# An attention-then-FFN kernel on one core: 512-token FFN tiles, one load queue in the order of need, v scaled on VectorE at first, scores inside the y step

## The chip, the cores and the metric

One core of one Trainium2 chip. The metric is the device time of one execution in microseconds (us), as the median of several runs. The traced span is 1.7 us shorter than the time of the same run (276.9 and 278.6 for the kernel before), so times are compared with times and spans with spans.

The names: PE is TensorE (the matmul engine), ACT is ScalarE, DVE is VectorE, POOL is GpSimd, SP is SyncE. A queue is the list of transfers that one engine issues; a transfer lands when its last data are in the core. Half clock is a stretch in which PE was granted about 0.5 of its full clock.

## The reference

A recurrent attention with a fixed decay per head, then a gated FFN over its output. Shapes: 4 batches, 8 heads, 768 positions, head size 64 (so 3072 tokens of width 512), inner width 1536, all float32.

```python
def _attn_ref(q, k, v):
    gamma = 1.0 - 2.0 ** (-5.0 - np.arange(H))
    for t in range(S):
        state = gamma * state + outer(k[:, :, t], v[:, :, t])     # (B,H,D,D)
        y[:, :, t] = scale * einsum('bhd,bhde->bhe', q[:, :, t], state)

def _moe_ref(x, w_gate, w_val, w_out):
    gate = 1.0 / (1.0 + np.exp(-(x @ w_gate)))
    return (gate * (x @ w_val)) @ w_out
```

The kernels process attention in chunks of 128 positions (6 per batch, 24 in all): scores within a chunk, a state carried from chunk to chunk, the decay put into scaled v on one side and into a table on the other.

## The kernel before

Per chunk there are three steps: `step_t` (k and q transposed on PE, copied by ACT), `step_s` (scores, masked by VectorE), `step_y` (state z, output y, evicted by VectorE with the decay table). Attention of batch b+1 is dealt out between the FFN groups of batch b. What matters is the first part: which queue gets which load, in which order, and where v is scaled.

```python
def load_chunk(b, c):                       # k, q cast to bf16 on POOL's queue, v as f32 on SyncE's
    ...
    nc.gpsimd.dma_start(out=kn[b, c], in_=k[b, :, rows, :]...)
    nc.gpsimd.dma_start(out=qn[b, c], in_=q[b, :, rows, :]...)
    nc.sync.dma_start(out=vf[b, c], in_=v[b, :, rows, :]...)      # 8 buffers of vf

def scale_v(b, c):
    vs[b, c] = ld.tile([C, H, D], BF16, tag="vs", name="vs", bufs=8)
    nc.gpsimd.tensor_tensor(vs[b, c], vf[b, c], tabv[...], op=ALU.mult)
...
for c in range(NCH): load_chunk(0, c)       # (cut: constants and tables between them)
for s in range(NFF // 2): load_gate_val(s)  # w_gate and w_val, 256 columns each, POOL's queue
for s in range(4): load_out(s)
for c in range(NCH): scale_v(0, c)          # POOL again: strictly behind its 28 DMA issues
for c in range(NCH): load_chunk(1, c)
for step in attention(0): step()            # six chunks before the first FFN group
for b in range(B):
    groups = ffn_groups(b)                  # 24 up groups of 384 columns, 6 down groups
    steps = attention(b + 1) if b + 1 < B else []
    ...                                     # scale_v(b + 1, ...), load_chunk(b + 2, ...)
    for i, g in enumerate(groups):
        g()
        upto = -(-len(steps) * (i + 1) // len(groups))
        while done < min(upto, len(steps)): steps[done](); done += 1
```

Of the kernel before, what the change touches and what calls it, by code (L numbers as in the profile page):

```python
# [9 lines left out]
F32 = mybir.dt.float32  # L10
BF16 = mybir.dt.bfloat16
I32 = mybir.dt.int32
AX = mybir.ActivationFunctionType
# [4 lines left out]
def kernel(  # L18
# [19 lines left out]
    HALF = S // 2  # L38
# [12 lines left out]

    qn, kn, vf = {}, {}, {}

    def load_chunk(b, c):
        rows = slice(c * C, (c + 1) * C)
        qn[b, c] = ld.tile([C, H, D], BF16, tag="qn", name="qn")
        kn[b, c] = ld.tile([C, H, D], BF16, tag="kn", name="kn")
        vf[b, c] = ld.tile([C, H, D], F32, tag="vf", name="vf", bufs=8)
        nc.gpsimd.dma_start(out=kn[b, c], in_=k[b, :, rows, :].rearrange("h s d -> s h d"))  # L59
        nc.gpsimd.dma_start(out=qn[b, c], in_=q[b, :, rows, :].rearrange("h s d -> s h d"))  # L60
        nc.sync.dma_start(out=vf[b, c], in_=v[b, :, rows, :].rearrange("h s d -> s h d"))
# [5 lines left out]
    def load_gate_val(s):  # L67
        cols = slice(s * 256, (s + 1) * 256)
        for dst, src in ((wg, moe_w_gate), (wv, moe_w_val)):
            nc.gpsimd.dma_start(out=dst[:, :, cols],  # L70
                                in_=src.rearrange("(kk p) n -> p kk n", p=128)[:, :, cols])

    def load_out(s):
# [3 lines left out]

    tokv = const.tile([128, NCH], I32, name="tokv")
    nc.gpsimd.iota(tokv, pattern=[[C, NCH]], base=0, channel_multiplier=1)
    ident = const.tile([128, 128], BF16, name="ident")  # L80
    make_identity(nc, ident)
    load_chunk(0, 0)
    toky = const.tile([128, S], I32, name="toky")
    nc.gpsimd.iota(toky, pattern=[[1, S]], base=0, channel_multiplier=0)  # L84
# [3 lines left out]
                            compare_op=ALU.is_ge, fill=0.0)  # L88

# [14 lines left out]
    for p in range(NP):  # L104
        nc.scalar.activation(taby[:, p, :], toky, AX.Exp, scale=lgp[:, p:p + 1], bias=lsc)
# [4 lines left out]
    for c in range(1, NCH):  # L110
        load_chunk(0, c)


    xT, vs, qkT, stA, stB, zps, zbd = {}, {}, {}, {}, {}, {}, {}

    def scale_v(b, c):
        vs[b, c] = ld.tile([C, H, D], BF16, tag="vs", name="vs", bufs=8)
        nc.gpsimd.tensor_tensor(vs[b, c], vf[b, c],  # L118
                                tabv[:, c, :].unsqueeze(2).to_broadcast([C, H, D]), op=ALU.mult)

    def step_t(b, c):
        tp = pa.tile([128, 2 * NP, C], BF16, tag="tp", name="tp")
        for i, src in enumerate((kn[b, c], qn[b, c])):
            for p in range(NP):
                nc.tensor.transpose(tp[:, i * NP + p, :],  # L125
                                    src[:, 2 * p:2 * p + 2, :].rearrange("s h d -> s (h d)"), ident)
        qkT[b, c] = at.tile([128, 2 * NP, C], BF16, tag="qkT", name="qkT")
        nc.scalar.activation(qkT[b, c], tp, AX.Copy)  # L128

    def step_s(b, c):  # L130
        t = qkT[b, c]
        sA = pa.tile([128, NP, C], F32, tag="sA", name="sA")
        sB = pa.tile([128, NP, C], F32, tag="sB", name="sB")
        for p in range(NP):
            nc.tensor.matmul(sA[:, p, :], t[0:D, p, :], t[0:D, NP + p, :], start=True, stop=True)  # L135
            nc.tensor.matmul(sB[:, p, :], t[D:128, p, :], t[D:128, NP + p, :], start=True, stop=True)  # L136
        stA[b, c] = at.tile([128, NP, C], BF16, tag="stA", name="stA")
        stB[b, c] = at.tile([128, NP, C], BF16, tag="stB", name="stB")
        nc.vector.tensor_tensor(stA[b, c], sA, causal4, op=ALU.mult)  # L139
        nc.vector.tensor_tensor(stB[b, c], sB, causal4, op=ALU.mult)  # L140

    def step_y(b, c):
        t = qkT[b, c]
        if c == 0:
            xT[b] = at.tile([128, NP, S], BF16, tag="xT", name="xT")
            zps[b] = pa.tile([128, NP, C], F32, tag="z", name="z")
        if c < NCH - 1:
            for p in range(NP):
                nc.tensor.matmul(zps[b][:, p, :],  # L149
                                 kn[b, c][:, 2 * p:2 * p + 2, :].rearrange("s h d -> s (h d)"),  # L150
                                 vs[b, c][:, 2 * p:2 * p + 2, :].rearrange("s h d -> s (h d)"),
                                 start=(c == 0 and p == 0), stop=True, skip_group_check=True)
        y = pa.tile([128, NP, C], F32, tag="y", name="y")
        if c > 0:
            for p in range(NP):
                nc.tensor.matmul(y[:, p, :], zbd[b, c - 1][:, p, :], t[:, NP + p, :],  # L156
                                 start=(p == 0), stop=False, skip_group_check=True)
        for p in range(NP):
            nc.tensor.matmul(y[0:D, p, :], vs[b, c][:, 2 * p, :], stA[b, c][:, p, :],  # L159
                             start=(c == 0 and p == 0), stop=True, skip_group_check=True)  # L160
            nc.tensor.matmul(y[D:128, p, :], vs[b, c][:, 2 * p + 1, :], stB[b, c][:, p, :],  # L161
                             start=(c == 0 and p == 0), stop=True, skip_group_check=True)
        if c < NCH - 1:
            zbd[b, c] = at.tile([128, NP, C], BF16, tag="zbd", name="zbd")
            nc.vector.tensor_tensor(zbd[b, c], zps[b], diag4, op=ALU.mult)  # L165
        cols = slice(c * C, (c + 1) * C)
        nc.vector.tensor_tensor(xT[b][:, :, cols], y, taby[:, :, cols], op=ALU.mult)  # L167

    def attention(b):
        steps = [lambda: step_t(b, 0), lambda: step_s(b, 0)]  # L170
        for c in range(NCH):
            if c + 1 < NCH:
                steps.append(lambda c=c: step_t(b, c + 1))
            steps.append(lambda c=c: step_y(b, c))
            if c + 1 < NCH:
                steps.append(lambda c=c: step_s(b, c + 1))
        return steps


    def ffn_groups(b):  # L180
        hT = ffn.tile([128, NFF, S], BF16, tag="hT", name="hT", bufs=2)

        def up(n1, hf):
            cols = slice(hf * HALF, (hf + 1) * HALF)
            ps = []
            for w in (wg, wv):
                t = pf.tile([128, 512], F32, tag="ff", name="ff")
                for kk in range(KT):
                    nc.tensor.matmul(t[:, 0:HALF], w[:, kk, n1 * 128:(n1 + 1) * 128], xT[b][:, kk, cols],  # L189
                                     start=(kk == 0), stop=(kk == KT - 1))  # L190
                ps.append(t)
            gs = ffn.tile([128, HALF], F32, tag="gs", name="gs")
            nc.scalar.activation(gs, ps[0][:, 0:HALF], AX.Sigmoid)  # L193
            nc.vector.tensor_tensor(hT[:, n1, cols], gs, ps[1][:, 0:HALF], op=ALU.mult)  # L194

        def down(sm):
            o = pf.tile([128, 512], F32, tag="ff", name="ff")
            for n1 in range(NFF):
                nc.tensor.matmul(o, hT[:, n1, sm * 128:(sm + 1) * 128], wo[:, n1, :],  # L199
                                 start=(n1 == 0), stop=(n1 == NFF - 1))  # L200
            ob = ffn.tile([128, D_MODEL], F32, tag="ob", name="ob")
            nc.scalar.copy(ob, o)  # L202
            row = b * S + sm * 128
            nc.sync.dma_start(out=out[row:row + 128, :], in_=ob)

        return ([lambda n1=n1, hf=hf: up(n1, hf) for n1 in range(NFF) for hf in range(2)]
                + [lambda sm=sm: down(sm) for sm in range(NCH)])


    for s in range(NFF // 2):  # L210
        load_gate_val(s)
    for s in range(4):
        load_out(s)
    for c in range(NCH):
        scale_v(0, c)
    for c in range(NCH):
        load_chunk(1, c)
    for step in attention(0):
        step()
    for b in range(B):  # L220
        groups = ffn_groups(b)
        steps = attention(b + 1) if b + 1 < B else []
        if b + 1 < B:
            for c in range(NCH):
                scale_v(b + 1, c)
        if b + 2 < B:
            for c in range(NCH):
                load_chunk(b + 2, c)
        done = 0
        for i, g in enumerate(groups):  # L230
            g()
            upto = -(-len(steps) * (i + 1) // len(groups))
            while done < min(upto, len(steps)):
                steps[done]()
                done += 1
# [30 lines left out]
```

## Time and profile before

| | before |
|---|---|
| time, median of 3 runs | 277.68 us (277.05 to 278.29) |
| traced span | 276.9 us |
| first FFN matmul | 51.1 us |
| PE waits for data after it | 2.4 us, then half clock |
| one batch (FFN beside attention) | 56.97 us of PE |

How to read it: the page gives busy tenths per engine in 40 equal slices, the chain of waits follows the last instruction back to what released it, the waits sum up who stood idle for whom. The prediction below shows the lines.

### The profile page before, as it was taken

To read this page: it belongs to the slowest core of one execution; us is meant where nothing else is said; L and a number is where in the kernel's file an instruction comes from. 1 tells how busy PE (TensorE), PEld (TensorE's weight loads), DVE (VectorE), ACT (ScalarE), POOL (GpSimd) and SP (SyncE) were. 2 spreads that over 40 slices of the span, in tenths; PEclk is the share of its full clock that TensorE was granted. 3 is DMA by queue.
4 is the path that set the end of the run, shared out by engine and by line. 5 is a ranking of instruction groups with operands and counts; after the bars stand their busy time and mean duration, and the time that the engine had idled before them with its cause. 6 is when DMAs were issued, how large, how long until landed. Compare 5 with 4: busy or idle time off the path is not lost.

```text
span 276.9 us, 4474 instructions
## 1 busy us (share of the span) xinstructions
PE 233.9 (84%) x1792; PEld 136.2 (49%) x1792; DVE 110.1 (40%) x200; ACT 91.4 (33%) x158; POOL 80.6 (29%) x98
## 2 busy tenths in 40 slices
PE   0400058599999999999999999999999999999994
PEld 0200046355666544566666445666665455665441
DVE  1100049546555512356567112656761314444100
ACT  6310014234444312444443214444243124333121
POOL 8836599359892970041011000000000000000000
PEclk9999999979999999999999999999999999999999
DMA  9999999999990999680000122000001220000122
GB/s 135 183 157 182 196 199 195 160 158 176 178 133 8 65 169 147 161 144 0 2 1 0 69 85 76 2 0 2 1 2 38 78 96 20 2 0 0 38 96 96
DMA packets 86293, 23.89 MB, mean 86 GB/s; under 512 B 75520, under 2 KB 83200, under 8 KB 86272
## 3 DMA queue, kind: packets, MB, share of 16 engines
q0 software_dynamic: 57856, 11.01, 47.8%
q1 hardware_dynamic: 28416, 12.59, 20.3%
q8 instruction: 14, 0.23, 0.4%
q14 instruction: 7, 0.06, 0.1%
HBM read 28.31 MB, written 6.29 MB: 125 GB/s over the span
## 4 chain that ended last, share of the span: by engine, by line
PE 79%; DMA 12%; POOL 7%; issue 1%; ACT 0%; POOLq 0%; ACTq 0%
PE ff L189 46%; PE ff L199 23%; DMA qn<-in_q_dram 9%; DMA wg<-in_moe_w_gate_dram 4%; PE tp L125 3%; POOL vs L118 2%; PE y L159 2%; PE sA L135 2%; POOL kn L59 2%; PE y L156 1%; PE z L149 1%; POOL qn L60 1%; POOL wo L74 1%; POOL wv L70 1%; POOL toky L84 0%
## 5 line engine op out<-in xcount | busy, mean ns | idle before, releaser
L194 DVE TENSOR_TENSOR hT<-gs,ff 128x384 bf16<-128x384 f32 x96 | 53.1, 554 | 75.2 <-PE ff L189 57.6
L189 PE MATMUL ff<-xT,wg 128*128 128x384 bf16 x384 | 79.1, 329 | 0.0
L189 PE MATMUL ff<-xT,wv 128*128 128x384 bf16 x384 | 78.8, 328 | 0.0
L193 ACT ACTIVATE gs<-ff 128x384 f32<-128x384 f32 x96 | 47.0, 489 | 78.6 <-PE ff L189 47.8
L199 PE MATMUL ff<-wo,hT 128*128 128x512 bf16 x288 | 64.4, 379 | 0.0
L189 PEld LDWEIGHTS <-wv 128*128 128x128 bf16 x384 | 37.8, 98 | 25.2 <-issue 0.7
L189 PEld LDWEIGHTS <-wg 128*128 128x128 bf16 x384 | 34.9, 98 | 22.6 <-issue 0.5
L199 PEld LDWEIGHTS <-hT 128*128 128x128 bf16 x288 | 27.3, 98 | 31.9
L128 ACT ACTIVATE qkT<-tp 128x1024 bf16<-128x1024 bf16 x24 | 24.6, 1023 | 48.0 <-PE tp L125 48.0
L118 POOL TENSOR_TENSOR vs<-vf,tabv 128x512 bf16<-128x512 f32 x24 | 24.4, 1042 | 45.4 <-PE y L161 17.3
L202 ACT COPY ob<-ff 128x512 f32<-128x512 f32 x24 | 14.0, 585 | 53.7 <-PE ff L199 51.7
L165 DVE TENSOR_TENSOR zbd<-z,diag 128x512 bf16<-128x512 f32 x20 | 13.7, 684 | 40.7 <-PE z L149 40.7
L149 PE MATMUL z<-vs,kn 128*128 128x128 bf16 x80 | 8.2, 228 | 23.7 <-POOL vs L118 23.7
L59 POOL DMA_DIRECT2D kn<-in_k_dram x24 | 22.0, 915 | 6.0 <-DMA kn<-in_k_dram 3.6
L60 POOL DMA_DIRECT2D qn<-in_q_dram x24 | 21.6, 902 | 5.3 <-DMA qn<-in_q_dram 3.6
L139 DVE TENSOR_TENSOR stA<-sA,causal 128x512 bf16<-128x512 f32 x24 | 16.4, 683 | 16.5 <-PE sB L136 16.5
L167 DVE TENSOR_TENSOR xT<-y,taby 128x512 bf16<-128x512 f32 x24 | 16.4, 682 | 14.5 <-PE y L161 14.5
L149 PEld LDWEIGHTS <-kn 128*128 128x128 bf16 x80 | 6.3, 103 | 26.1 <-issue 23.9
L125 PE MATMUL tp<-ident,kn 128*128 128x128 bf16 x96 | 10.0, 230 | 8.0 <-DMA kn<-in_k_dram 8.0
L140 DVE TENSOR_TENSOR stB<-sB,causal 128x512 bf16<-128x512 f32 x24 | 16.3, 679 | 0.0
L125 PE MATMUL tp<-ident,qn 128*128 128x128 bf16 x96 | 10.2, 233 | 4.1 <-DMA qn<-in_q_dram 4.1
L125 PEld LDWEIGHTS <-kn 128*128 128x128 bf16 x96 | 7.2, 102 | 11.2 <-DMA kn<-in_k_dram 8.3
(34 smaller groups left out, 108.8 us busy)
## 6 DMA issues: line engine op xcount, KB each, us to landing
vf<-in_v_dram SPq DMA_DIRECT2D x24, 256.0 KB, 8.9
out_dram<-ob SPq DMA_DIRECT2D x24, 256.0 KB, 2.0
kn<-in_k_dram POOLq DMA_DIRECT2D x24, 128.0 KB, 8.5
qn<-in_q_dram POOLq DMA_DIRECT2D x24, 128.0 KB, 8.5
wg<-in_moe_w_gate_dram POOLq DMA_DIRECT2D x6, 256.0 KB, 10.1
wv<-in_moe_w_val_dram POOLq DMA_DIRECT2D x6, 256.0 KB, 10.0
wo<-in_moe_w_out_dram POOLq DMA_DIRECT2D x4, 384.0 KB, 13.2
```

The costliest lines, as they stand in the source:

```text
L59: nc.gpsimd.dma_start(out=kn[b, c], in_=k[b, :, rows, :].rearrange("h s d -> s h d"))
L60: nc.gpsimd.dma_start(out=qn[b, c], in_=q[b, :, rows, :].rearrange("h s d -> s h d"))
L118: nc.gpsimd.tensor_tensor(vs[b, c], vf[b, c], tabv[:, c, :].unsqueeze(2).to_broadcast([C, H, D]), op=ALU.mult)
L125: nc.tensor.transpose(tp[:, i * NP + p, :], src[:, 2 * p:2 * p + 2, :].rearrange("s h d -> s (h d)"), ident)
L128: nc.scalar.activation(qkT[b, c], tp, AX.Copy)
L139: nc.vector.tensor_tensor(stA[b, c], sA, causal4, op=ALU.mult)
L149: nc.tensor.matmul(zps[b][:, p, :], kn[b, c][:, 2 * p:2 * p + 2, :].rearrange("s h d -> s (h d)"), vs[b, c][:, 2 * p:2 * p + 2, :].rearran ...
L167: nc.vector.tensor_tensor(xT[b][:, :, cols], y, taby[:, :, cols], op=ALU.mult)
L189: nc.tensor.matmul(t[:, 0:HALF], w[:, kk, n1 * 128:(n1 + 1) * 128], xT[b][:, kk, cols], start=(kk == 0), stop=(kk == KT - 1))
L193: nc.scalar.activation(gs, ps[0][:, 0:HALF], AX.Sigmoid)
L194: nc.vector.tensor_tensor(hT[:, n1, cols], gs, ps[1][:, 0:HALF], op=ALU.mult)
L199: nc.tensor.matmul(o, hT[:, n1, sm * 128:(sm + 1) * 128], wo[:, n1, :], start=(n1 == 0), stop=(n1 == NFF - 1))
```

## The change

Its intent: start the FFN after four chunks of attention, not six; bring in each piece of data just before it is needed; keep the scaling of v off POOL's queue of DMA issues while that is long; put the scores of the next chunk inside the y step. The core of the diff:

```diff
+    def load_chunk(g):                     # g counts chunks over all batches
+        load_kq(g)
+        load_v(g, nc.gpsimd)               # v now on POOL's queue too
...
+    for g in range(4):
+        load_v(g, nc.sync)                 # only v of chunks 0 to 3 stays on SyncE's queue
+    load_kq(0) ... load_kq(3)              # (cut: constants between them)
...
+        eng = nc.vector if g < 8 else nc.gpsimd       # in step_t(g)
+        eng.tensor_tensor(vs[g], vf[g], tabv[...], op=ALU.mult)
...
-    def step_y(b, c):
+    def step_y(g, nxt=None):               # z, first half of y, then:
+        evict = step_s(nxt) if nxt is not None else None
...                                         # second half of y, evictions
-        def up(n1, hf):                    # 24 groups of 384 columns per batch
+        def up(n1):                        # 12 groups of 512 columns per tile of four chunks
...
-    for s in range(NFF // 2):
+    for s in range(3):
         load_gate_val(s)
+    load_chunk(4)
+    for s in range(3, NFF // 2):
+        load_gate_val(s)
+    load_chunk(5)
     for s in range(4):
         load_out(s)
-    for c in range(NCH):
-        scale_v(0, c)
-    for c in range(NCH):
-        load_chunk(1, c)
-    for step in attention(0):
+    load_chunk(6)
+    load_chunk(7)
+    first = attention(0)                   # chunks 0 to 3
+    first[0]()
+    for p in range(NP):
+        make_taby(p)                       # decay tables on ACT, behind the first copy
+    for step in first[1:]:
         step()
```

More of the change, by code (lines that the diff above doesn't have):

```diff
@@ L37 @@
     NFF = D_FF // 128
-    HALF = S // 2
     scale = 1.0 / math.sqrt(D)
@@ L49, with src, load_v, load_kq @@
     pf = ctx.enter_context(tc.tile_pool(name="pf", bufs=3, space=bass.MemoryType.PSUM))
+    NG = B * NCH
+    NT = N_TOK // 512
     qn, kn, vf = {}, {}, {}
-    def load_chunk(b, c):
-        rows = slice(c * C, (c + 1) * C)
-        qn[b, c] = ld.tile([C, H, D], BF16, tag="qn", name="qn")
-        kn[b, c] = ld.tile([C, H, D], BF16, tag="kn", name="kn")
-        vf[b, c] = ld.tile([C, H, D], F32, tag="vf", name="vf", bufs=8)
-        nc.gpsimd.dma_start(out=kn[b, c], in_=k[b, :, rows, :].rearrange("h s d -> s h d"))
-        nc.gpsimd.dma_start(out=qn[b, c], in_=q[b, :, rows, :].rearrange("h s d -> s h d"))
-        nc.sync.dma_start(out=vf[b, c], in_=v[b, :, rows, :].rearrange("h s d -> s h d"))
+    def src(x, g):
+        b, c = divmod(g, NCH)
+        return x[b, :, c * C:(c + 1) * C, :].rearrange("h s d -> s h d")
+    def load_v(g, eng):
+        vf[g] = ld.tile([C, H, D], F32, tag="vf", name="vf", bufs=8)
+        eng.dma_start(out=vf[g], in_=src(v, g))
+    def load_kq(g):
+        kn[g] = ld.tile([C, H, D], BF16, tag="kn", name="kn")
+        qn[g] = ld.tile([C, H, D], BF16, tag="qn", name="qn")
+        nc.gpsimd.dma_start(out=kn[g], in_=src(k, g))
+        nc.gpsimd.dma_start(out=qn[g], in_=src(q, g))
+    def load_chunk(g):
+        load_kq(g)
+        load_v(g, nc.gpsimd)
     wg = wpool.tile([128, KT, D_FF], BF16, name="wg")
@@ L68, in load_gate_val @@
         cols = slice(s * 256, (s + 1) * 256)
-        for dst, src in ((wg, moe_w_gate), (wv, moe_w_val)):
+        for dst, w in ((wg, moe_w_gate), (wv, moe_w_val)):
             nc.gpsimd.dma_start(out=dst[:, :, cols],
-                                in_=src.rearrange("(kk p) n -> p kk n", p=128)[:, :, cols])
+                                in_=w.rearrange("(kk p) n -> p kk n", p=128)[:, :, cols])
     def load_out(s):
@@ L75, in load_out @@
                             in_=moe_w_out.rearrange("(n p) d -> p n d", p=128)[:, s * 3:(s + 1) * 3, :])
+    for g in range(4):
+        load_v(g, nc.sync)
+    load_kq(0)
+    ident = const.tile([128, 128], BF16, name="ident")
+    make_identity(nc, ident)
+    load_kq(1)
     tokv = const.tile([128, NCH], I32, name="tokv")
     nc.gpsimd.iota(tokv, pattern=[[C, NCH]], base=0, channel_multiplier=1)
-    ident = const.tile([128, 128], BF16, name="ident")
-    make_identity(nc, ident)
-    load_chunk(0, 0)
-    toky = const.tile([128, S], I32, name="toky")
-    nc.gpsimd.iota(toky, pattern=[[1, S]], base=0, channel_multiplier=0)
     causal = const.tile([128, 128], F32, name="causal")
@@ L88 @@
                             compare_op=ALU.is_ge, fill=0.0)
+    load_kq(2)
+    toky = const.tile([128, S], I32, name="toky")
+    nc.gpsimd.iota(toky, pattern=[[1, S]], base=0, channel_multiplier=0)
+    load_kq(3)
     tabv = const.tile([128, NCH, H], F32, name="tabv")
@@ L103, with make_taby @@
     taby = const.tile([128, NP, S], F32, name="taby")
-    for p in range(NP):
+    def make_taby(p):
         nc.scalar.activation(taby[:, p, :], toky, AX.Exp, scale=lgp[:, p:p + 1], bias=lsc)
@@ L108, with pair, step_t, step_s @@
     diag4 = diag.unsqueeze(1).to_broadcast([128, NP, 128])
-    for c in range(1, NCH):
-        load_chunk(0, c)
-    xT, vs, qkT, stA, stB, zps, zbd = {}, {}, {}, {}, {}, {}, {}
-    def scale_v(b, c):
-        vs[b, c] = ld.tile([C, H, D], BF16, tag="vs", name="vs", bufs=8)
-        nc.gpsimd.tensor_tensor(vs[b, c], vf[b, c],
-                                tabv[:, c, :].unsqueeze(2).to_broadcast([C, H, D]), op=ALU.mult)
-    def step_t(b, c):
+    xT, vs, qkT, stA, stB, zbd = {}, {}, {}, {}, {}, {}
+    zps = {}
+    def pair(t, p):
+        return t[:, 2 * p:2 * p + 2, :].rearrange("s h d -> s (h d)")
+    def step_t(g):
         tp = pa.tile([128, 2 * NP, C], BF16, tag="tp", name="tp")
-        for i, src in enumerate((kn[b, c], qn[b, c])):
+        for i, x in enumerate((kn[g], qn[g])):
             for p in range(NP):
-                nc.tensor.transpose(tp[:, i * NP + p, :],
-                                    src[:, 2 * p:2 * p + 2, :].rearrange("s h d -> s (h d)"), ident)
-        qkT[b, c] = at.tile([128, 2 * NP, C], BF16, tag="qkT", name="qkT")
-        nc.scalar.activation(qkT[b, c], tp, AX.Copy)
-    def step_s(b, c):
-        t = qkT[b, c]
+                nc.tensor.transpose(tp[:, i * NP + p, :], pair(x, p), ident)
+        qkT[g] = at.tile([128, 2 * NP, C], BF16, tag="qkT", name="qkT")
+        nc.scalar.activation(qkT[g], tp, AX.Copy)
+        vs[g] = ld.tile([C, H, D], BF16, tag="vs", name="vs", bufs=4)
+        eng = nc.vector if g < 8 else nc.gpsimd
+        eng.tensor_tensor(vs[g], vf[g], tabv[:, g % NCH, :].unsqueeze(2).to_broadcast([C, H, D]),
+                          op=ALU.mult)
+    def step_s(g):
+        t = qkT[g]
         sA = pa.tile([128, NP, C], F32, tag="sA", name="sA")
@@ L136, in step_s, with evict @@
             nc.tensor.matmul(sB[:, p, :], t[D:128, p, :], t[D:128, NP + p, :], start=True, stop=True)
-        stA[b, c] = at.tile([128, NP, C], BF16, tag="stA", name="stA")
-        stB[b, c] = at.tile([128, NP, C], BF16, tag="stB", name="stB")
-        nc.vector.tensor_tensor(stA[b, c], sA, causal4, op=ALU.mult)
-        nc.vector.tensor_tensor(stB[b, c], sB, causal4, op=ALU.mult)
-    def step_y(b, c):
-        t = qkT[b, c]
+        stA[g] = at.tile([128, NP, C], BF16, tag="stA", name="stA")
+        stB[g] = at.tile([128, NP, C], BF16, tag="stB", name="stB")
+        def evict():
+            nc.vector.tensor_tensor(stA[g], sA, causal4, op=ALU.mult)
+            nc.vector.tensor_tensor(stB[g], sB, causal4, op=ALU.mult)
+        return evict
+    def step_y(g, nxt=None):
+        b, c = divmod(g, NCH)
+        if g % 4 == 0:
+            xT[g // 4] = at.tile([128, NP, 512], BF16, tag="xT", name="xT")
         if c == 0:
-            xT[b] = at.tile([128, NP, S], BF16, tag="xT", name="xT")
             zps[b] = pa.tile([128, NP, C], F32, tag="z", name="z")
@@ L148, in step_y @@
             for p in range(NP):
-                nc.tensor.matmul(zps[b][:, p, :],
-                                 kn[b, c][:, 2 * p:2 * p + 2, :].rearrange("s h d -> s (h d)"),
-                                 vs[b, c][:, 2 * p:2 * p + 2, :].rearrange("s h d -> s (h d)"),
+                nc.tensor.matmul(zps[b][:, p, :], pair(kn[g], p), pair(vs[g], p),
                                  start=(c == 0 and p == 0), stop=True, skip_group_check=True)
@@ L155, in step_y @@
             for p in range(NP):
-                nc.tensor.matmul(y[:, p, :], zbd[b, c - 1][:, p, :], t[:, NP + p, :],
+                nc.tensor.matmul(y[:, p, :], zbd[g - 1][:, p, :], qkT[g][:, NP + p, :],
                                  start=(p == 0), stop=False, skip_group_check=True)
+        evict = step_s(nxt) if nxt is not None else None
         for p in range(NP):
-            nc.tensor.matmul(y[0:D, p, :], vs[b, c][:, 2 * p, :], stA[b, c][:, p, :],
+            nc.tensor.matmul(y[0:D, p, :], vs[g][:, 2 * p, :], stA[g][:, p, :],
@@ L160, in step_y @@
                              start=(c == 0 and p == 0), stop=True, skip_group_check=True)
-            nc.tensor.matmul(y[D:128, p, :], vs[b, c][:, 2 * p + 1, :], stB[b, c][:, p, :],
+            nc.tensor.matmul(y[D:128, p, :], vs[g][:, 2 * p + 1, :], stB[g][:, p, :],
                              start=(c == 0 and p == 0), stop=True, skip_group_check=True)
         if c < NCH - 1:
-            zbd[b, c] = at.tile([128, NP, C], BF16, tag="zbd", name="zbd")
-            nc.vector.tensor_tensor(zbd[b, c], zps[b], diag4, op=ALU.mult)
@@ L166, in step_y @@
-        cols = slice(c * C, (c + 1) * C)
-        nc.vector.tensor_tensor(xT[b][:, :, cols], y, taby[:, :, cols], op=ALU.mult)
-    def attention(b):
-        steps = [lambda: step_t(b, 0), lambda: step_s(b, 0)]
-        for c in range(NCH):
-            if c + 1 < NCH:
-                steps.append(lambda c=c: step_t(b, c + 1))
-            steps.append(lambda c=c: step_y(b, c))
-            if c + 1 < NCH:
-                steps.append(lambda c=c: step_s(b, c + 1))
-        return steps
-    def ffn_groups(b):
-        hT = ffn.tile([128, NFF, S], BF16, tag="hT", name="hT", bufs=2)
-        def up(n1, hf):
-            cols = slice(hf * HALF, (hf + 1) * HALF)
+            zbd[g] = at.tile([128, NP, C], BF16, tag="zbd", name="zbd")
@@ new lines, in step_y, with attention @@
+            nc.vector.tensor_tensor(zbd[g], zps[b], diag4, op=ALU.mult)
+        if evict:
+            evict()
+        col = (g % 4) * C
+        nc.vector.tensor_tensor(xT[g // 4][:, :, col:col + C], y, taby[:, :, c * C:(c + 1) * C], op=ALU.mult)
+    def attention(t):
+        g = 4 * t
+        return [lambda: step_t(g), lambda: step_s(g)(), lambda: step_t(g + 1), lambda: step_y(g, g + 1),
+                lambda: step_t(g + 2), lambda: step_y(g + 1, g + 2), lambda: step_t(g + 3),
+                lambda: step_y(g + 2, g + 3), lambda: step_y(g + 3)]
@@ L185, in up, with ffn_groups @@
+    def ffn_groups(t):
+        hT = ffn.tile([128, NFF, 512], BF16, tag="hT", name="hT", bufs=2)
+        def up(n1):
             ps = []
             for w in (wg, wv):
-                t = pf.tile([128, 512], F32, tag="ff", name="ff")
+                u = pf.tile([128, 512], F32, tag="ff", name="ff")
                 for kk in range(KT):
-                    nc.tensor.matmul(t[:, 0:HALF], w[:, kk, n1 * 128:(n1 + 1) * 128], xT[b][:, kk, cols],
+                    nc.tensor.matmul(u, w[:, kk, n1 * 128:(n1 + 1) * 128], xT[t][:, kk, :],
@@ L190, in up @@
                                      start=(kk == 0), stop=(kk == KT - 1))
-                ps.append(t)
-            gs = ffn.tile([128, HALF], F32, tag="gs", name="gs")
-            nc.scalar.activation(gs, ps[0][:, 0:HALF], AX.Sigmoid)
-            nc.vector.tensor_tensor(hT[:, n1, cols], gs, ps[1][:, 0:HALF], op=ALU.mult)
+                ps.append(u)
+            gs = ffn.tile([128, 512], F32, tag="gs", name="gs")
+            nc.scalar.activation(gs, ps[0], AX.Sigmoid)
+            nc.vector.tensor_tensor(hT[:, n1, :], gs, ps[1], op=ALU.mult)
@@ L202, in down @@
             nc.scalar.copy(ob, o)
-            row = b * S + sm * 128
+            row = t * 512 + sm * 128
             nc.sync.dma_start(out=out[row:row + 128, :], in_=ob)
-        return ([lambda n1=n1, hf=hf: up(n1, hf) for n1 in range(NFF) for hf in range(2)]
-                + [lambda sm=sm: down(sm) for sm in range(NCH)])
-    for s in range(NFF // 2):
+        return [lambda n1=n1: up(n1) for n1 in range(NFF)] + [lambda sm=sm: down(sm) for sm in range(4)]
+    for s in range(3):
         load_gate_val(s)
+    load_chunk(4)
+    for s in range(3, NFF // 2):
+        load_gate_val(s)
+    load_chunk(5)
     for s in range(4):
         load_out(s)
-    for c in range(NCH):
-        scale_v(0, c)
-    for c in range(NCH):
-        load_chunk(1, c)
-    for step in attention(0):
-        step()
-    for b in range(B):
-        groups = ffn_groups(b)
-        steps = attention(b + 1) if b + 1 < B else []
-        if b + 1 < B:
-            for c in range(NCH):
-                scale_v(b + 1, c)
-        if b + 2 < B:
-            for c in range(NCH):
-                load_chunk(b + 2, c)
+    load_chunk(6)
[5 more added lines that the diff above has]
+    for step in first[1:]:
+        step()
+    for t in range(NT):
+        groups = ffn_groups(t)
+        steps = attention(t + 1) if t + 1 < NT else []
+        if t + 2 < NT:
+            for g in range(4 * t + 8, 4 * t + 12):
+                load_chunk(g)
         done = 0
-        for i, g in enumerate(groups):
-            g()
+        for i, group in enumerate(groups):
+            group()
             upto = -(-len(steps) * (i + 1) // len(groups))
```

## The prediction

> **What bounds the kernel now.** I read the busy slices of the page first, then the chain of work that ended last, then the waits, then the order of time on POOL, last the table of stretches. The slices:
>
> ```profile
> PE   0400058599999999999999999999999999999994
> POOL 8836599359892970041011000000000000000000
> PEclk9999999979999999999999999999999999999999
> DMA  9999999999990999680000122000001220000122
> ```
>
> A slice is 6.9 us. PE is full from the ninth slice on; before that it is nearly idle while the transfers are full. So there are two stages: some 55 us of start, bound by what is loaded and in which order, and 220 us bound by PE. The chain shows PE's stage and its unit costs:
>
> ```profile
> 43.38 11.91 DMA qn<-in_q_dram
> ...
> 112.58 1.30 PE ff L189 x8
> ...
> 169.55 1.30 PE ff L189 x8
> ...
> 226.52 31.20 PE ff L189 x192
> 257.72 15.55 PE ff L199 x72
> ...
> 273.34 0.58 ACT ob L202
> ```
>
> The last batch runs without attention beside it: 31.20/192 = 0.1625 us per 384-column up matmul, 15.55/72 = 0.216 us per 512-column down matmul, 46.75 us per batch. The pieces at 112.58 and 169.55 begin two successive batches: 56.97 us apart, of which 46.75 is FFN, so six chunks of attention take 10.2 us of PE, 1.70 each. What fills the start is in the waits:
>
> ```profile
> PE z L149 <- POOL vs L118: 23.7, 1, 23.7
> ...
> PE tp L125 <- DMA kn<-in_k_dram: 8.0, 2, 7.3
> ...
> PE tp L125 <- DMA qn<-in_q_dram: 4.1, 3, 1.7
> ```
>
> and on POOL, in order of time:
>
> ```profile
> 34.31 0.76 POOL L74 DMA_DIRECT2D wo<-in_moe_w_out_dram  x1 [0.58 <-DMA wg<-in_moe_w_gate_dram]
> 35.65 0.77 POOL L74 DMA_DIRECT2D wo<-in_moe_w_out_dram  x1 [0.58 <-DMA wv<-in_moe_w_val_dram]
> 36.44 6.04 POOL L118 TENSOR_TENSOR vs<-vf,tabv 128x512 bf16<-128x512 f32 x6
> ```
>
> The first v was in the core at 4.1 us (the trace records each landing), but its scaling stands behind 28 DMA issues in POOL's strict order and starts at 36.4. PE waits 23.7 us for it, runs attention of six chunks from 37.6 to 51.1, does one FFN group, then waits 0.63 and 1.74 us for chunk 0 of the next batch, queued behind all weights, and runs at half clock after that wait. The stretches give the transfer rates and the clock:
>
> ```profile
> 16.00:20.00 4.00, 0.00 (x0) 0.00 (x0) 0.00 (x0) 0.00 (x0) 1.36 (x3) 1.00 1.69 158
> 32.00:36.00 4.00, 0.00 (x0) 0.00 (x0) 0.00 (x0) 0.00 (x0) 2.24 (x4) 1.00 1.45 196
> 56.00:60.00 4.00, 4.00 (x23) 1.95 (x22) 1.42 (x3) 1.74 (x3) 1.36 (x3) 0.65 1.69 157
> ```
>
> The last two columns but one are clock and DMA share, the last GB/s: 158 with k, q and v beside each other, 196 with weights alone, clock 0.65 after the wait.
>
> Check of the model: first FFN group 51.1, FFN 768 x 0.1625 + 288 x 0.216 = 187.0, attention 18 x 1.70 = 30.6, waits 2.4, slow clock some 1.4, tail from 273.3 to 276.9 = 3.6. Sum 276.1 against 276.9 seen.
>
> **What the Trainium skill says.** (1) "TensorE: Matmul & The Clock Gate", section "Wait — 56ns, not 53.3ns?": warm, a matmul of N columns costs N/2.4 GHz and some 2.5 ns, 215.7 at 512; 384 gives 162.5. The trace agrees: 216 and 162.5. (2) Same page, "Part 1: The HAM clock gate (the "warmup" mystery)": PE starts at half clock and needs about 3.4 us of activity. The trace agrees in kind (0.65 in that stretch; one group took 1.28 us per half and not 0.65). (3) "DMA: Bandwidth & Descriptors", "Issuing engines are not separate DMA queues": all issuers share the same 16 engines, so moving v to another queue buys no bandwidth; only the order changes. The trace agrees: with v beside them k and q land some 2.1 us apart, without it some 0.85. (4) "GPSIMD Engine Reference", "3.1 Elementwise — side-by-side cycle accounting": elementwise work is about half as fast there as on VectorE. The trace has 1042 ns on POOL for the v scaling; a DVE op of that shape (with a PSUM input) takes 683 ns and starts 0.60 after the one before.
>
> **The change part by part.**
>
> *512-token tiles.* The up step goes from 768 matmuls of 384 columns to 576 of 512: 124.8 us becomes 576 x 0.216 = 124.4. Down is unchanged at 62.2. So FFN is 186.6, a saving of 0.4 us. The longer DVE products (96 x 554 ns become 72 of some 684) and sigmoids (96 x 489 become 72 of some 585) lie beside PE, which takes 8 x 0.216 = 1.73 us per group. The tile matters for the start: four chunks, not six, before the first FFN.
>
> *Scores inside the y step.* One switch between kinds of matmul fewer per chunk. In the order of time each switch leaves some 0.1 us in which PE starts nothing. 20 chunks: 1.5 to 2 us.
>
> *v scaled on DVE for eight chunks.* Takes away the 23.7 us wait. Adds 0.6 us of DVE per chunk in the first attention, which is DVE-bound already (four ops, 2.39 us per chunk): now five, 3.0.
>
> *Loading order.* From the landings: k or q alone 0.85 us each, weights 1.34 us per 256 KB, v on its own 1.1 to 1.4, taken as 1.25; while v0 to v3 share the engines, k and q need 2.1. v0 to v3 in by about 10.5; kq0 by 9.0; kq3 by 15.2; then two weight pieces per slice: slice 0 at 17.9, slice 2 at 23.2; chunk 4 at 26.2; slice 5 at 34.2; chunk 5 at 37.2 (its q 35.9); w_out, 4 x 2.0, 45.2; chunk 6 at 48.1 (its q 46.9); chunk 7 at 51.
>
> *First attention.* kq0 at 9.0, transposes 9.6, copy on ACT to 10.7. Then the four decay tables stand on ACT (4 x 0.95 = 3.8 us) before the second copy: to 14.5, second copy to 15.5. Scores of chunk 1 at 15.5, and from there DVE sets the pace: three ops of y(0), then two rounds of five, two at the end, with small latencies between. xT complete at about 25.4. FFN starts at 25.5, not 51.1.
>
> *First FFN tile.* Sum without a wait for data: 25.5 + 186.6 + 20 x 1.70 + 3.6 + 1.4 of slow clock = 251.1. But the tile needs chunk 5 after four groups (about 35; its q lands 35.9) and chunk 6 after eight (about 44; its q lands 46.9, behind w_out). So PE transposes chunk 6 at about 47.4. Left then: FFN 186.6 - 8 x 1.73 = 172.8; attention 20 x 1.70 less about 3 done = 31; tail 3.6; slow clock after that wait 1.3. Sum 256.1, less 1.5 for the switches: a span of 254.6. The median of the times lies 0.8 above the traced span before. I take **254 us**, a little under that sum, since v alone on one queue may pack better than I assumed.
>
> **The rivals.**
> - *The transfers are hidden*: v goes faster without a second queue beside it, or PE arrives later than I think; PE is bound from 25 us on. For it: the share of overlapping packets is 1.45 for one queue and 1.7 to 1.9 for two at a lower rate. Against: 256-byte pieces are small in either queue. Time 249 to 251.
> - *The load becomes the wait in place of the scaling*: v generated by POOL costs more than 1.25 us, POOL's issues of some 0.9 us add up (eight more in the first tile), or VectorE's scaling, which reads two SBUF tensors, disturbs POOL's descriptors. And a v that lands late now blocks VectorE's strict order, so an FFN product waits behind it and PE's three PSUM buffers run out. For it: transfers run without a pause until 50 us in my table, and POOL is seen waiting for earlier transfers to drain. Time 260 to 266.
> - *VectorE as bound in steady state*: a burst of four attention ops (2.4 us) ahead of an FFN product. Against: DVE was busy 23.72 of 39 us in the stretch of 113 to 152, about as much as it will be, and a group of 1.73 us with three buffers leaves over a microsecond of slack. If wrong, 20 x 0.5 = 10 us.
> - *Nothing gained*: the start is just the bytes. Against: of 28.3 MB read, the first tile's first group needs four chunks and one weight slice only. I give this little.
>
> **Range and chances.** The gain of 23 us is 25.6 us of earlier start, less two chunks of attention moved into PE's stage (2 x 1.70 = 3.4), less some 2 of added wait for chunks 5 and 6, plus 0.4 and 1.5 to 2, and rounding. The start may be 22 to 28, the wait 0 to 9. Range 247 to 263. Faster by over 2% means under 272.1; only a wait of 18 us in the first tile would miss it: 0.96, within 2% 0.03, slower 0.01.
>
> **What would show it right or wrong.** The first FFN matmul at 24 to 27 us (a start past 30 refutes the first-attention step); no PE wait for POOL's v scaling; five DVE ops per chunk at 3.0 us in the first attention; PE waits for k or q of chunks 5 and 6 of 1 to 5 us in total, and none after 60 us; up matmuls 0.216 apart; 1.6 to 1.7 us of PE per chunk from tile 1 on; the last tile 31.0 us of PE. If PE is idle more than 2 us after 60 us, the steady-state step is wrong; if v lands over 1.6 us apart from what was issued before it, the transfer table is wrong.

## The result, and the profile after

| | before | after |
|---|---|---|
| time, median of 4 runs | 277.99 us (277.05 to 279.36) | 254.15 us (253.87 to 254.49) |
| ratio | | 0.9139 (95%: 0.9098 to 0.9181) |
| traced span | 276.9 us | 252.2 us |
| first FFN matmul | 51.1 us | 26.5 us |
| PE waits for k and q after it | 2.4 us | 0.66 us |

A ratio here is the mean time of one kernel's runs over the mean time of the other's runs of the same rounds, so it is not quite the ratio of the medians in the table.

The busy slices of the changed kernel, each now 6.3 us:

```profile
PE   0356899899999999999999999999999999999993
POOL 7985674888899301891101101101100000000000
PEclk9999799999999999999999999999999999999999
DMA  9999999999999902799002200002200002200022
```

PE is nearly full from the fifth slice on, where before it took until the ninth. The transfers are full for the first 80 us, as they were: no bytes were saved, they came in another order. The start in order of time, first ACT, then VectorE, then PE (start, duration, instruction, and in brackets the idle time before it with what ended it):

```profile
10.46 1.02 ACT L139 ACTIVATE qkT<-tp 128x1024 bf16<-128x1024 bf16 x1 [3.81 <-PE tp L137]
11.38 3.77 ACT L121 ACTIVATE taby<-toky,lsc,lgp 128x768 f32<-128x768 int32 x4
15.05 1.00 ACT L139 ACTIVATE qkT<-tp 128x1024 bf16<-128x1024 bf16 x1
```

```profile
16.75 0.69 DVE L156 TENSOR_TENSOR stA<-sA,causal 128x512 bf16<-128x512 f32 x1 [2.01 <-PE sB L151]
...
20.07 0.69 DVE L156 TENSOR_TENSOR stA<-sA,causal 128x512 bf16<-128x512 f32 x1 [0.24 <-PE sB L151]
...
23.07 0.68 DVE L156 TENSOR_TENSOR stA<-sA,causal 128x512 bf16<-128x512 f32 x1
...
25.78 0.69 DVE L187 TENSOR_TENSOR xT<-y,taby 128x512 bf16<-128x512 f32 x1 [0.23 <-PE y L179]
```

```profile
26.52 1.27 PE L204 MATMUL ff<-xT,wg 128*128 128x512 bf16 x3 [0.79 <-DVE xT L187]
...
44.91 0.40 PE L137 MATMUL tp<-ident,kn 128*128 128x128 bf16 x4 [0.19 <-DMA kn<-in_k_dram]
45.78 0.40 PE L137 MATMUL tp<-ident,qn 128*128 128x128 bf16 x4 [0.47 <-DMA qn<-in_q_dram]
```

The second copy on ACT stands behind the decay tables (11.38 to 15.15). From there VectorE sets the pace: the masking of chunks 1, 2 and 3 begins at 16.75, 20.07 and 23.07, 3.3 and 3.0 us apart, then the FFN starts. PE's only waits for data after that are the two at chunk 6 of 0.19 and 0.47 us. The stretch in which PE runs below full clock (the last three columns are clock, DMA share and GB/s):

```profile
28.00:32.00 4.00, 4.00 (x20) 2.06 (x18) 1.29 (x2) 1.98 (x3) 2.36 (x4) 0.68 1.46 196
66.63:217.03 150.40, 149.40 (x1049) 76.87 (x1068) 69.61 (x109) 52.66 (x80) 38.59 (x41) 1.00 0.43 66
```

The second line spans the four tiles in the middle: 150.40 us, 37.60 each. A tile's FFN is 144 matmuls of 0.216 us, 31.1 us, so attention takes 37.60 - 31.1 = 6.5 us per four chunks, 1.63 per chunk, against 1.70 before.

### The profile page after: what moved, and what is told of

It reads as the page before. It is cut to its first block, busy times and chain, and to the rows that moved or that the text cites. A ratio compares the mean times of both kernels' runs of the same rounds, so it can differ in the third digit from the quotient of the medians.

```text
span 252.2 us, 3949 instructions
## 1 busy us (share of the span) xinstructions
PE 230.0 (91%) x1572; PEld 118.2 (47%) x1600; DVE 111.0 (44%) x184; ACT 86.5 (34%) x134; POOL 90.5 (36%) x110
## 4 chain that ended last, share of the span: by engine, by line
PE 79%; DMA 11%; POOL 5%; issue 2%; ACT 1%; ACTq 0%; POOLq 0%
PE ff L204 44%; PE ff L214 25%; DMA qn<-in_q_dram 4%; DMA wv<-in_moe_w_val_dram 4%; DMA wg<-in_moe_w_gate_dram 3%; PE tp L137 3%; PE y L177 2%; PE sA L150 2%; POOL kn L66 2%; PE y L173 1%; POOL qn L67 1%; PE z L168 1%; POOL wg L80 1%; POOL wv L80 1%; ACT ob L217 1%
## 5 line engine op out<-in xcount | busy, mean ns | idle before, releaser
L209 DVE TENSOR_TENSOR hT<-gs,ff 128x512 bf16<-128x512 f32 x72 | 49.4, 687 | 82.9 <-PE ff L204 82.9
L204 PE MATMUL ff<-xT,wv 128*128 128x512 bf16 x284 | 74.4, 383 | 0.5
L204 PE MATMUL ff<-xT,wg 128*128 128x512 bf16 x273 | 72.8, 381 | 1.4 <-DVE xT L187 0.8
L208 ACT ACTIVATE gs<-ff 128x512 f32<-128x512 f32 x72 | 42.9, 596 | 70.5 <-PE ff L204 70.0
L204 PEld LDWEIGHTS <-wv 128*128 128x128 bf16 x288 | 28.4, 99 | 34.4 <-issue 0.8
L142 POOL TENSOR_TENSOR vs<-vf,tabv 128x512 bf16<-128x512 f32 x16 | 16.7, 1050 | 72.8 <-PE y L179 67.7
L204 PEld LDWEIGHTS <-wg 128*128 128x128 bf16 x288 | 26.2, 98 | 27.9 <-issue 1.0
L61 POOL DMA_DIRECT2D vf<-in_v_dram x20 | 18.3, 914 | 2.7 <-issue 1.3
L137 PEld LDWEIGHTS <-kn 128*128 128x128 bf16 x96 | 7.5, 104 | 13.3 <-DMA kn<-in_k_dram 8.0
L150 PE MATMUL sA<-qkT 64*128 64x128 bf16 x96 | 10.1, 229 | 3.8 <-ACT qkT L139 3.8
```

Of the source, the lines that this page charges most:

```text
L61: eng.dma_start(out=vf[g], in_=src(v, g))
L137: nc.tensor.transpose(tp[:, i * NP + p, :], pair(x, p), ident)
L142: eng.tensor_tensor(vs[g], vf[g], tabv[:, g % NCH, :].unsqueeze(2).to_broadcast([C, H, D]), op=ALU.mult)
L204: nc.tensor.matmul(u, w[:, kk, n1 * 128:(n1 + 1) * 128], xT[t][:, kk, :], start=(kk == 0), stop=(kk == KT - 1))
L208: nc.scalar.activation(gs, ps[0], AX.Sigmoid)
L209: nc.vector.tensor_tensor(hT[:, n1, :], gs, ps[1], op=ALU.mult)
```

## The experiments

The theory going in was that of the prediction: the whole gain is in the start, and it needs both an early scaling of v and loads in the order of need; the steady stage gains little. The rivals were that one part alone (the scaling, the order or the smaller tile) gives it. All kernels gave correct results.

### 1. The kernel before with the scaling alone (b_dve)

```diff
 def scale_v(b, c):
-    nc.gpsimd.tensor_tensor(vs[b, c], vf[b, c], ...)
+    eng = nc.vector if b == 0 else nc.gpsimd
+    eng.tensor_tensor(vs[b, c], vf[b, c], ...)
 # and scale_v(0, c) is called in step_t(0, c), not in a loop behind the weights
```

> The kernel before with one part alone: v of the first batch is scaled on VectorE, chunk by chunk; tiles, order and queues of the loads stay. Theory (both waits must go, scaling and order): attention of the first batch now ends near 30 us instead of 51, but the second FFN group waits for k and q of the next batch, which stand behind all weights and land near 51 to 55 us, so the wait moves from the scaling to the loads and the time falls by only 1 to 4 us, to 274-277. Rival (the scaling was the bound): the time falls by 20 us or more.

Measured: 283.26 us (283.07 to 284.22), ratio to before 1.0203 (1.0157 to 1.0249). Slower by 1.6 to 2.5%: with a limit of 2% the verdict is "unclear", but no gain is left. The first FFN matmul came at 34.4 us and not at 51.1, but PE then stood still:

```profile
59.31 0.61 PE L126 MATMUL tp<-ident,kn 128*128 128x128 bf16 x4 [22.21 <-DMA kn<-in_k_dram]
```

The wait moved from the scaling to k of the next batch, as the theory said; that the time would still fall a little was wrong. k of that chunk landed at 59.3 us, where before it landed at 53.2. The landings tell why: an early scaling frees the eight v buffers early, and SyncE's queue at once fetched six more chunks of v, four of the next batch and two of the one after; they landed at 23.8, 28.7, 33.0, 37.2, 41.4 and 45.7 us, between the other loads. Before, those came after 49 us. They were needed by nobody yet, and took the engines from the weights (last w_val at 50.7 us, before 40.7) and from k and q behind them.

### 2. The kernel before with the order alone (b_order)

```diff
     for s in range(NFF // 2):
         load_gate_val(s)
+        if s < 2:
+            load_chunk(1, s)
```

> The kernel before with the order alone: k and q of two chunks of the next batch go between the first weight slices; v is still scaled on POOL after the weights. Theory: the wait for k and q at 53 to 55 us goes (2.4 us and the slow clock after it, 1.4 us), but the scaling starts some 4 us later, near 40 us, so the time stays within 2 us of before. Rival (order of the loads is the bound): 5 us or more off.

Measured: 277.85 us (276.99 to 279.94), ratio 1.0017 (0.9956 to 1.0078): the same. The first FFN matmul came at 54.6 us and PE waited for nothing after it. What the order gave back (2.4 us of wait and the half clock after it) the later scaling took.

### 3. Both of these together (b_both)

The diff of the first, and `load_chunk(1, s)` after each of the first five weight slices.

> The kernel before, 768-token batches and v on its own queue as they were, with both: v of the first batch scaled on VectorE and one chunk's k and q of the next batch after each weight slice. Theory (these two parts are the gain and the 512-token tile adds little): FFN starts near 30 us against 26.4 with the change, but two chunks fewer (2 x 1.7 us) lie in PE's stage, so 253 to 258 us. Rival (the smaller tile is what gives the early start): 262 us or more.

Measured: 274.91 us (273.78 to 275.66), ratio 0.9892 (0.9845 to 0.9938): about 1% faster. The expectation was missed by 17 us. First FFN matmul at 35.1 us, and then:

```profile
59.03 0.59 PE L152 MATMUL z<-vs,kn 128*128 128x128 bf16 x4 [12.12 <-POOL vs L119]
```

```profile
55.27 0.77 POOL L74 DMA_DIRECT2D wo<-in_moe_w_out_dram  x1 [0.55 <-DMA wv<-in_moe_w_val_dram]
56.12 0.91 POOL L59 DMA_DIRECT2D kn<-in_k_dram  x1
57.02 0.89 POOL L60 DMA_DIRECT2D qn<-in_q_dram  x1
57.92 3.06 POOL L119 TENSOR_TENSOR vs<-vf,tabv 128x512 bf16<-128x512 f32 x3
```

I had moved the scaling of the first batch only. That of the second was still on POOL, behind all issues, and the old wait stood there again, one batch later. It fits this that the change scales eight chunks on VectorE and not four. v of the later batches was again fetched ahead on its own queue (six chunks, landed from 23.5 to 41.0 us).

### 4. Everything of the change but the tile and the scores (b_all)

```diff
+        eng = nc.sync if b == 0 and c < 4 else nc.gpsimd     # v on the one queue
+        eng.dma_start(out=vf[b, c], ...)
...
+    eng = nc.vector if b < 2 else nc.gpsimd                  # v of two batches scaled on VectorE
...                                                           # load_chunk(1, s) after each weight slice
```

> The kernel before with its 768-token batches and its order of steps, but v of batches 0 and 1 scaled on VectorE, chunks of batch 1 between the weight slices, and v of all but the first four chunks on the one queue. Theory (these are the gain, the tile of 512 adds at most 2 us): FFN starts near 29 us, two chunks fewer lie in PE's stage, 252 to 257 us. Rival (the tile of four chunks is what the early start needs): 260 us or more.

Measured: 253.51 us (252.94 to 254.46), ratio 0.9127 (0.9090 to 0.9164), where the changed kernel has 0.9139 and, in another call, 0.9158. So the 768-token batches with the old steps do just as well. The first FFN matmul is 2.2 us later than with the change, and PE waits for no data after it:

```profile
28.75 0.50 PE L193 MATMUL ff<-xT,wg 128*128 128x384 bf16 x1
```

A batch takes 56.97 us of PE as before. By these numbers, what the tile gains at the start (2.2 us), and what the new steps save (20 chunks at 0.08 us), goes into two more chunks that lie in PE's stage (2 x 1.70 us); no run separates the tile from the steps. (This kernel also keeps the decay tables early on ACT and spreads the chunks more evenly between the weights than the change does, so it bounds the worth of tile and scores together and is not a pure undoing of them.)

### 5. The changed kernel with the scaling on POOL (a_pool)

```diff
-        eng = nc.vector if g < 8 else nc.gpsimd
+        eng = nc.gpsimd
```

> The changed kernel with the scaling of v on POOL for all chunks, as before. Theory: the first scaling stands behind the DMA issues up to chunk 7, which end at 41.3 us, so FFN starts near 53 us against 26.5, and the whole later course shifts by it: 275 to 281 us, the gain gone. Rival (early scaling matters little, the loads and the tile do it): under 262 us.

Measured: 279.18 us (278.61 to 280.78), ratio 1.0057. First FFN matmul at 53.8 us, as expected near 53. The first scaling starts at 41.20:

```profile
40.29 0.89 POOL L61 DMA_DIRECT2D vf<-in_v_dram  x1 [0.64 <-DMA wo<-in_moe_w_out_dram]
41.20 4.04 POOL L142 TENSOR_TENSOR vs<-vf,tabv 128x512 bf16<-128x512 f32 x4
```

Without this part nothing of the gain is left. It is necessary, as long as POOL issues the loads in this order; experiment 1 shows that it is not sufficient.

### 6. The changed kernel with the order undone (a_late)

All weight slices and w_out before chunks 4 to 7.

> The changed kernel with only the order of need undone: all weight slices and w_out are loaded before chunks 4 to 7. Theory: k of chunk 4 lands near 41 us against 24.3, PE has done one FFN group by then and waits some 12 us, all weights are there after that: 262 to 268 us. Rival (transfers are hidden behind PE anyway): within 2 us of 254.

Measured: 265.57 us (265.14 to 266.28), ratio 0.9553. First FFN matmul at 26.3 us as with the change; then the expected wait, where 12 had been estimated:

```profile
40.40 0.61 PE L137 MATMUL tp<-ident,kn 128*128 128x128 bf16 x4 [10.49 <-DMA kn<-in_k_dram]
```

Nearly half of the gain hangs on where the loads of two chunks, 4 and 5, stand.

### 7. The changed kernel with v on SyncE's queue (a_spv)

```diff
 def load_chunk(g):
     load_kq(g)
-    load_v(g, nc.gpsimd)
+    load_v(g, nc.sync)
```

> The changed kernel with all v on SyncE's queue instead of the one queue. Theory (a second queue has no order against the first, so v of chunks 4 to 11 is fetched ahead as soon as buffers are free and holds up k, q and weights): k and q of chunk 3 land near 21 us against 15.6, weights and chunks 5 and 6 later by some 5 us, 257 to 263 us. Rival (queues only save issue time, order does not matter): within 1.5 us of 254.

Measured: 265.69 us (264.84 to 265.84), ratio 0.9556, worse than I expected. q of chunk 3 landed at 21.7 us against 15.6 with the change. v of chunks 4 to 11 all landed by 38.7 us; chunk 4, which PE needed first, had its k at 37.1:

```profile
37.12 0.61 PE L137 MATMUL tp<-ident,kn 128*128 128x128 bf16 x4 [5.69 <-DMA kn<-in_k_dram]
```

The bytes are the same. A second queue has no place in the order of the first: it runs as far ahead as its buffers let it. (This is read from the landings; no run held the second queue back, by fewer buffers for instance.)

### 8. Scores in a step of their own (a_split)

```diff
-        return [step_t(g), step_s(g), step_t(g+1), step_y(g, g+1), step_t(g+2), ...]   # 9 steps per tile
+        return [step_t(g), step_s(g), step_t(g+1), step_y(g), step_s(g+1), ...]        # 12 steps per tile
```

> The changed kernel with the scores of the next chunk again in a step of their own. Theory: one more switch between kinds of matmul per chunk, some 0.08 us each for 20 chunks, 1.5 us more: 255 to 256.5 us, 1.70 us of PE per chunk against 1.62. Rival (the switch costs nothing and the lower cost per chunk has another cause): within 0.4 us of 254.15.

Measured: 258.02 us (257.39 to 258.76), ratio 0.9290. The middle tiles take, in the same view as above,

```profile
69.44:221.13 151.69, 150.63 (x1050) 75.89 (x1069) 70.68 (x109) 52.68 (x80) 36.21 (x39) 1.00 0.39 62
```

151.69/4 = 37.92 against 37.60 us: 0.32 per tile, 0.08 per chunk, as expected. But the time rose by 3.9 us and not by 1.5. The rest is not the switch. With twelve steps dealt out over sixteen groups, the transposes of chunk 5 come after the third group and not after the fourth, before the data is there:

```profile
34.66 0.61 PE L137 MATMUL tp<-ident,kn 128*128 128x128 bf16 x4 [3.40 <-DMA kn<-in_k_dram]
```

and PE then ran at half clock for a while (the first up matmuls after it took twice as long).

### 9. The changed kernel again, and scores behind y in the same step (after_again, a_split9)

> The changed kernel once more, so that the three kernels beside it have it on the same chip: 253.5 to 255 us, ratio to before near 0.914.

> The changed kernel with the scores after the y matmuls, in the same step (nine steps per tile, as with the change), instead of between the two halves of y. Theory: the number of switches of matmul kind is the same, so PE's cost per chunk stays 1.62 us (the 12-step variant had 1.70); FFN starts some 1.5 us earlier, since y of chunk 0 no longer waits for the copy of chunk 1 that stands behind the decay tables on ACT, but the wait for k of chunk 5 takes that back: within 1 us of the changed kernel. Rival (scores inside y save the cost per chunk by themselves): 1.70 us per chunk again and 1.6 us more.

```diff
-        lambda: step_y(g, g + 1)                            # scores between the two halves of y
+        lambda: (step_y(g), step_s(g + 1)())                # scores after y, still nine steps
```

Measured, on one chip with 5 rounds: the changed kernel 254.19 us (253.92 to 254.43), ratio 0.9158 (0.9132 to 0.9183); the variant 254.11 us (254.03 to 254.20), the same ratio and interval. The tiles take 37.60 us in both. So the place of the scores inside the y step is worth nothing; that they share a step with y, and don't stand alone between FFN groups, is worth the 0.08 us per chunk.

The repeat brought one more thing. Its FFN started at 25.45 us and not at 26.5, and the start of the variant was 25.07 (I had expected 1.5 us of difference, it was 0.4). The waits for k and q of chunks 5 and 6 rose from 0.66 us to 1.9 and 2.1, and the time did not move. From the fourth group to the eighth the loads set the pace, and a start that is a microsecond earlier is given back there.

### 10. Two versions of my own (a_best, a_best9)

```diff
+    toky, tokv iota                # first on POOL, so that ACT makes the decay tables before any copy
     load_kq(0); ident; load_v(0); load_chunk(1); ...; load_chunk(3)    # v behind its k and q, one queue
...
+    load_gate_val(0); load_chunk(4); load_gate_val(1); load_gate_val(2); load_chunk(5)
+    load_gate_val(3); load_gate_val(4); load_chunk(6); load_gate_val(5)
+    load_out(0); load_chunk(7); load_out(1); load_out(2); load_out(3)
```

> A version of my own: decay tables first on ACT, v right behind its k and q on the one queue from chunk 0 on, chunks 4 to 7 spread more evenly between weight slices, w_out last; steps as in the changed kernel. Theory (the start is the chain of loads, first attention and its DVE pace, with chunks 5 and 6 as the next wait): k and q of chunk 0 land near 6.5 us against 9.8, FFN starts at 20 to 22 us against 26.5, no wait for chunks 5 and 6, some 2.5 us for the last parts of w_out: 247 to 251 us. Rival (the load of chunk 6 and the weights sets the end, whatever the order): within 1.5 us of 254.

> The same with the scores after the y matmuls in the same step. Theory: y of chunk 0 no longer waits for chunk 1, FFN starts another 0.5 to 1.5 us earlier where DVE is not the pace: 0 to 1.5 us below the version with the scores inside y. Rival: no difference, since DVE sets the pace either way.

Measured on the same chip as experiment 9: 250.14 us (249.73 to 250.40), ratio 0.9011 (0.8986 to 0.9037), and with the scores behind y 249.83 us (249.52 to 250.21), ratio 0.9005 (0.8979 to 0.9031). Both beat the changed kernel by 4 us (0.9005/0.9158 = 0.983); they don't differ from each other clearly. q of chunk 0 landed at 6.75 us (9.8 with the change), the FFN started at 22.9 and 22.3 us, a little later than I expected, and chunks 5 and 6 were waited for no more. The one data wait left, in the second version, is 0.67 us for w_out, where I had estimated 2.5. Which of the edits (tables, v behind its k and q, even spread) brings the 4 us was not separated. The slices of the second:

```profile
PE   0688999989999999999999999999999999999993
POOL 8998677767899922961111001111000000000000
```

## Why the prediction was right

The time was forecast as 254 and measured as 254.15 us. That it is so close is partly luck (see the sum below). By its steps:

- **The first attention** was right. q of chunk 0 was put at 9.0 us and landed at 9.8; the second copy on ACT at 15.5, it ended at 16.05; five VectorE ops per chunk at 3.0 us, seen 3.3 and 3.0; FFN at 25.5, seen 26.5 and in the repeat 25.45. No PE wait for POOL's scaling was left.
- **The table of loads** was right to about a microsecond: q of chunk 3 at 15.2 (15.6), second half of slice 0 at 17.9 (18.0), q of chunk 5 at 35.9 (35.7), w_out at 45.2 (43.9), q of chunk 6 at 46.9 (45.7). v on POOL's queue took 0.8 to 1.3 us where 1.25 was assumed, and w_out 1.9 a part where 2.0 was.
- **The first tile** was right in kind. The wait sat at chunk 6, as the table said, but it was 0.66 us, where the sum has about 3.7 and the list of signs 1 to 5 for chunks 5 and 6: this sign was missed here and met in the repeat (1.9). The loads of chunk 6 came 1.2 us earlier and the FFN started 1.0 later than put down. The second stretch of half clock (1.3 us) did not come: after this wait the granted clock stayed at 1.00 (44.7 to 46.5 us).
- **The steady stage** was right: 0.216 us per up matmul, 1.63 us of attention per chunk (1.70 less 0.08), no PE wait after 60 us.
- **The sum** was 2.4 us too high: 254.6 us of span were worked out and 252.2 seen. The wait was 3.0 us shorter and the second half clock 1.3; against this the FFN started 1.0 later, and the other 0.9 is in smaller terms (the tail after the last matmul, for one, took 3.9 us and not 3.6). The step from span to time was wrong too: it is 1.7 us in both profiled runs (278.6 and 276.9 before, 253.87 and 252.2 after), not 0.8, and 254 was then taken 0.6 below the span that had been worked out. That sum with 1.7 added gives 256.3 us: the working is good to some 2 us, and the agreement to 0.2 us is luck.
- **The rivals.** VectorE did not become the bound. Its scaling did not visibly disturb POOL either: a DMA issue for k took 911 ns on average, before 915. One part of the second rival was seen: VectorE stood idle for 1.5 us until v of chunk 6 landed (47.0 us), but PE did not stop for it. That the gain is "25.6 us of earlier start less two chunks moved into PE's stage" was the right account, and experiment 4 fits its second half: with 768-token batches the start is 2.2 us later and two chunks fewer lie in PE's stage, and the time is the same.

What the prediction did not see is how the parts depend on each other. It put the 23.7 us down to the scaling. Alone, the scaling makes the kernel 2% slower (experiment 1), the order alone does nothing (2), both together give 1% while the second batch is scaled on POOL and v runs ahead on its own queue (3), and only all three together give the 24 us (4). It said of the queue only that the order changes; that was worth 11.5 us (265.69 against 254.15). It put the saving of the scores under their place inside the y step. The reason that it gave, one switch between kinds of matmul fewer per chunk, fits 8 and 9; the place doesn't matter, since the scores save as much behind y in the same step.

Still open: whether v could stay on POOL if its scaling were put between the DMA issues, which no run tried; and how much of b_all's standing is due to its early decay tables and its finer order, and how much to the batch size; and what a second queue that cannot run ahead would cost.

## What to carry to other kernels

A start that is bound by loads has a list of waits, one behind the other: taking away the first shows the second, and its data can even come later, because buffers come free sooner and another queue fills them (k at 59.3 us and not 53.2 in experiment 1). Before moving a load to a second queue, ask what will stop it from running ahead of what is needed first; buffers are the only thing that did here. Work that depends on early data should not stand in the strict order of an engine that issues the late data's transfers, and this holds for every batch that is loaded in that stretch, not only for the first.

## What the Trainium skill lacked or had wrong

- "DMA: Bandwidth & Descriptors", "Issuing engines are not separate DMA queues", says that issuing from several engines only saves issue time. The runs show that it can also cost: v on a second queue made the changed kernel 11.5 us slower (265.69 against 254.15), by running ahead of k, q and weights; the section has no word on this, and no page gives its cost. Nor does the page give POOL's time per issue for many small pieces: POOL was busy 0.74 us per weight transfer of 512 pieces and some 0.9 per k, q or v of 1024 pieces. In the kernel before, the 28 issues ahead of the first scaling took 23.0 of the 36.4 us, and POOL's waits for earlier transfers between them 9.9.
- No page has the cost of loads that cast small pieces: k or q (256-byte reads, 128-byte writes, 128 KB written) took mostly 0.8 to 0.95 us each between landings on the one queue, not much less than v with the same number of pieces, no cast and twice the written bytes (0.8 to 1.3 us); the weights, cast in 512-byte writes, ran at 196 GB/s written.
- "GPSIMD Engine Reference", "3.1 Elementwise — side-by-side cycle accounting", gives 1.96 times VectorE's time for 2048 float32, and has no shorter operands for that operation. For the 512-column scaling of v with bf16 output the changed kernel's trace has medians of 1042 ns on POOL and 684 ns on VectorE, 1.52 times.
